# Attending the first batch whole before the feed-forward, with weights taken column by column

## The chip, the cores and the metric

The kernel runs on one core of one Trainium2 chip. The metric is the device time in microseconds (us). Most executions of a kernel agree within a few tenths of a per cent; a run that lies over 1.5% above the fastest of its kernel is called slow, and comparisons use the fast runs. TensorE's clock is at times halved; the records give the granted clock for any stretch, as a share of full speed (0.50 in some stretches below, the first from 44.90 to 51.73 us in the run with the old order). This record begins only when the clock is first released, at 10.71 us in the kernel before. What lies earlier is shown as 1.00, although the same pair of 503-column matmuls takes 1.05 us at 7.78 and 0.59 at 11.03.

## The reference

Two parts, one after the other, in float32:

```python
# 4 batches, 8 heads, 768 positions, 64 per head; 4 sink positions, window of 128
scores = q @ k.T / sqrt(64)
keep   = (key < 4) | ((query - key >= 0) & (query - key < 128))
a      = softmax(where(keep, scores, -1e9))
x      = (a @ v)                      # heads side by side: 3072 tokens x 512
out    = (relu(x @ w_gate) * (x @ w_val)) @ w_out     # 512 -> 1536 -> 512
```

Any token of the feed-forward needs all eight heads of its batch, so no feed-forward work on batch 0 can start before all heads of at least the first tokens are attended.

## The kernel before

It works in bf16. Attention goes in units of two heads. A unit is loaded, cast by GpSimd, transposed on TensorE (`T`), scored in groups of columns (`S`, exponential on ScalarE), multiplied with the values and the sums (`V`), and normalised on VectorE (`norm`). The feed-forward goes in chunks: one of 12 columns of weights for half a batch, 8 matmuls of 384 columns. The second product (`ffn2`) gathers 12 matmuls into one tile of 128 tokens.

```python
def chunk(b, c0, n, m):                     # first product, 4 + 4 matmuls
    for ko in range(KO):
        nc.tensor.matmul(out=gp, lhsT=wg[:, ko, m*128:(m+1)*128], rhs=x[:, ko, c0:c0+n], ...)
    nc.scalar.activation(gs, gp, Act.Relu)
    for ko in range(KO):
        nc.tensor.matmul(out=vp, lhsT=wv[:, ko, m*128:(m+1)*128], rhs=x[:, ko, c0:c0+n], ...)
    nc.vector.tensor_tensor(hT[:, m, c0:c0+n], gs, vp, op=Alu.mult)

def ffn2(b, t, m, tail=False):              # second product, one of 12 matmuls of a tile
    nc.tensor.matmul(out=op, lhsT=hTs[b][:, m, t*128:(t+1)*128], rhs=wo[:, m, :],
                     start=m == 0, stop=m == FM - 1)
    if m == FM - 1:
        nc.scalar.copy(ot[:], op)           # then stored
```

To start the feed-forward early, batch 0 is cut into two kinds of units, "L" (the first 376 tokens of two heads) and "M" (the other 392). The four L units come first, with filler matmuls ("warm") between them. The M units and the full "F" units of the other batches follow as stages between the chunks, at a pace given by PLAN (pairs of chunk number and stages done by then):

```python
for p in range(NP):                          # the front, cut
    U[p].S(0); ...; U[p].S(1)
    if p + 2 < NP: U[p + 2].T(*GV)
    warm(8)
    if p >= 1: norm(U[p - 1], 0, ps_gv)
...
ORDER = [(0, h, m) for h in range(2) for m in range(FM)]   # all 12 columns for one half, then the other
PLAN = ((0, 0), (2, 0), (10, 19), (23, 43), (47, 67), (71, 89), (72, 90))
for ci, (b, h, m) in enumerate(ORDER):
    while si < min(total, want(ci)):
        stages[si](); si += 1
    chunk(b, c0, n, m)
    left = FM - ci % FM
    for _ in range((len(f2) + left - 1) // left):   # second product spread evenly
        f2.popleft()()
```

Batch 0 gets its causal masks by an extra matmul before the scores; later batches by a multiplication on VectorE. The weights are loaded by GpSimd in four quarters of columns, the output weights in three thirds of rows, one third after the casts of each of three successive units.

The softmax here doesn't subtract the row's maximum and nothing guards it: scores larger than these inputs give would overflow.

## Time and profile before

The median is 276.26 us over four runs (275.64 to 277.87). Cutting the profiled span by TensorE's own timeline gives a table that the rest of this text uses. In the view of windows of the kernel before, each line has the stretch, its length, the busy time of each engine with its number of instructions (TensorE, weight load, VectorE, ScalarE, GpSimd), the granted clock, the DMA share and GB/s:

```profile
0.00:22.77 22.77, 17.71 (x189) 11.53 (x190) 12.84 (x37) 10.70 (x22) 19.18 (x45) 1.00 1.10 223
22.77:91.47 68.70, 63.52 (x653) 38.44 (x652) 48.28 (x113) 41.65 (x65) 32.03 (x53) 1.00 0.90 202
91.47:261.48 170.01, 170.01 (x1280) 94.73 (x1279) 86.49 (x180) 74.83 (x128) 16.59 (x26) 1.00 0.21 66
261.48:273.90 12.42, 8.58 (x40) 3.72 (x38) 0.55 (x1) 2.38 (x5) 0.00 (x0) 0.99 0.23 84
```

The first number is the stretch's length, the second TensorE's busy time; their difference is its idle time: 5.06, 5.18, 0 and 3.84 us. In the long third stretch TensorE never pauses. So there are two ways to win: take matmuls out, or take idle time out of the first 91 us.

### The profile page before, as it was taken

Reading aid. Unit: us, or ns where it says so; the run is one execution under the profiler, and the core shown is the slowest. Engines: PE = TensorE matmul, PEld = TensorE weight load, DVE = VectorE, ACT = ScalarE, POOL = GpSimd, SP = SyncE. Lnnn points to the kernel's source line nnn. Section 1 sums busy time; section 2 is a strip of 40 time slices with the busy share of each in tenths; the row PEclk is TensorE's granted clock in tenths of the full one; section 3 lists DMA queues with packets and bytes.
Section 4 is the critical chain, followed back from the end, with each engine's and each line's share of the span. In section 5 each row is a group of like instructions: output and inputs, shape, how many; then the busy total and the mean of one; then the engine's idle time right before and its main releaser. Section 6 shows DMA issues by size and latency. Waiting matters only on the chain.

```text
span 273.9 us, 5552 instructions
## 1 busy us (share of the span) xinstructions
PE 259.8 (95%) x2158; PEld 148.4 (54%) x2158; DVE 148.2 (54%) x329; ACT 129.6 (47%) x218; POOL 67.8 (25%) x123
## 2 busy tenths in 40 slices
PE   5997899899989999999999999999999999999994
PEld 4564555555545555555565555555655555555541
DVE  2486355778797755465666646565474722222210
ACT  3743656666646544536435363644535333323321
POOL 7973547653441330030402105000000000000000
PEclk9999999999999999999999999999999999999999
DMA  8999999998465170531707125101101110011122
GB/s 196 260 224 207 246 255 231 254 251 189 114 172 162 54 212 10 159 84 44 209 4 212 41 75 142 38 0 41 38 2 38 41 38 10 28 42 38 38 77 78
DMA packets 46858, 31.20 MB, mean 114 GB/s; under 512 B 28400, under 2 KB 43760, under 8 KB 46832
## 3 DMA queue, kind: packets, MB, share of 16 engines
q1 hardware_dynamic: 40224, 25.93, 34.2%
q0 software_dynamic: 5808, 4.72, 11.0%
q8 instruction: 17, 0.28, 0.4%
q10 hardware_dynamic: 800, 0.20, 0.3%
q14 instruction: 9, 0.07, 0.1%
HBM read 29.26 MB, written 6.29 MB: 130 GB/s over the span
## 4 chain that ended last, share of the span: by engine, by line
PE 84%; DVE 8%; ACT 3%; issue 1%; DMA 1%; POOL 1%; SPq 0%; DVEq 0%; ACTq 0%
PE gp L323 22%; PE op L342 22%; PE vp L329 21%; PE ops L248 7%; PE sps L226 5%; PE sps L221 2%; DVE R L311 2%; PE tkq L180 2%; DVE R L308 2%; PE tkq L183 2%; DVE xT L313 2%; ACT ee L230 2%; DMA stg<-in_q_dram 1%; DVE ee L232 1%; DVE rc L309 1%
## 5 line engine op out<-in xcount | busy, mean ns | idle before, releaser
L326 ACT ACTIVATE gs<-gp 128x384 f32<-128x384 f32 (+2 forms) x96 | 47.3, 493 | 73.2 <-PE gp L323 71.4
L323 PE MATMUL gp<-xT,wg 128*128 128x384 bf16 (+2 forms) x384 | 78.8, 327 | 1.4 <-DVE xT L313 1.4
L331 DVE TENSOR_TENSOR hT<-gs,vp 128x384 bf16<-128x384 f32 (+2 forms) x96 | 52.7, 549 | 49.3 <-PE vp L329 42.1
L329 PE MATMUL vp<-xT,wv 128*128 128x384 bf16 (+2 forms) x384 | 78.1, 326 | 0.0
L342 PE MATMUL op<-wo,hT 128*128 128x512 bf16 x288 | 75.9, 379 | 0.0
L230 ACT ACTIVATE ee<-sps 128x1006 bf16<-128x1006 f32 (+4 forms) x52 | 46.3, 905 | 26.5 <-PE sps L226 26.5
L329 PEld LDWEIGHTS <-wv 128*128 128x128 bf16 x384 | 37.6, 98 | 26.4 <-issue 1.6
L323 PEld LDWEIGHTS <-wg 128*128 128x128 bf16 x384 | 32.5, 98 | 25.2 <-issue 4.3
L342 PEld LDWEIGHTS <-hT 128*128 128x128 bf16 x288 | 28.2, 98 | 25.1
L232 DVE TENSOR_TENSOR ee<-ee,msk 128x1006 bf16<-128x1006 bf16 (+2 forms) x36 | 26.0, 723 | 26.0 <-ACT ee L230 25.8
L153 POOL CAST kn<-stg 128x768 bf16<-128x768 f32 (+2 forms) x20 | 15.4, 768 | 72.9 <-DMA stg<-in_k_dram 48.7
L346 ACT COPY ot<-op 128x512 f32<-128x512 f32 x24 | 14.1, 586 | 21.6 <-PE op L342 21.5
L308 DVE STREAM_TRANSPOSE R<-ops 128x384 f32<-128x384 f32 (+1 forms) x28 | 16.4, 584 | 14.3 <-PE ops L248 14.3
L186 ACT COPY kT<-tkq 128x768 bf16<-128x768 bf16 (+2 forms) x20 | 14.0, 700 | 18.1 <-PE tkq L183 17.9
L157 POOL CAST vn<-stg 128x768 bf16<-128x768 f32 (+2 forms) x20 | 14.4, 720 | 22.7 <-DMA stg<-in_v_dram 16.7
L311 DVE STREAM_TRANSPOSE R<-rc 128x384 f32<-128x384 f32 (+1 forms) x32 | 18.6, 582 | 1.1
L248 PEld LDWEIGHTS <-ones 128*64 128x64 bf16 x280 | 12.1, 109 | 12.3 <-issue 7.4
L313 DVE TENSOR_TENSOR xT<-ops,R 128x384 bf16<-128x384 f32 (+2 forms) x32 | 17.8, 557 | 1.4
L226 PEld LDWEIGHTS <-kT 64*128 64x128 bf16 x136 | 6.6, 93 | 19.2 <-issue 16.8
L248 PE MATMUL ops<-ee,ones 128*64 128x251 bf16 (+9 forms) x256 | 14.3, 238 | 2.2 <-DVE xT L313 1.3
L226 PE MATMUL sps<-qT,kT 64*128 64x251 bf16 (+3 forms) x136 | 15.5, 250 | 0.8 <-ACT qT L188 0.8
L153 POOL CAST qn<-stg 128x768 bf16<-128x768 f32 (+2 forms) x20 | 14.5, 724 | 5.2 <-DMA stg<-in_q_dram 4.8
(53 smaller groups left out, 169.8 us busy)
## 6 DMA issues: line engine op xcount, KB each, us to landing
out_dram<-ot SPq DMA_DIRECT2D x24, 256.0 KB
stg<-in_k_dram SPq DMA_DIRECT2D x12, 384.0 KB
stg<-in_q_dram SPq DMA_DIRECT2D x12, 384.0 KB
stg<-in_v_dram SPq DMA_DIRECT2D x24, 192.0 KB
wg<-in_moe_w_gate_dram POOLq DMA_DIRECT2D x4, 384.0 KB, 9.7
wv<-in_moe_w_val_dram POOLq DMA_DIRECT2D x4, 384.0 KB, 11.8
wo<-in_moe_w_out_dram POOLq DMA_DIRECT2D x3, 512.0 KB, 5.9
stg<-in_k_dram SPq DMA_DIRECT2D x4, 280.0 KB
```

The costliest lines, as they stand in the source:

```text
L153: cp(dst[0:pp, 0:nn, :, :], self.staging(what)[0:pp, :, :].rearrange("p h (n d) -> p n h d", d=64))
L226: nc.tensor.matmul(out=ps[:, h, c:c + w], lhsT=self.kw(j, r), rhs=qT[s][r, qa:qa + w], start=not biased, stop=True, skip_group_check=True)
L230: nc.scalar.activation(x, ps[:, :, 0:c], Act.Exp, bias=0.0, scale=scale)
L232: nc.vector.tensor_tensor(x, x, bc(msk[:, m0:m0 + c], 2), op=Alu.mult)
L248: nc.tensor.matmul(out=ps[1 - what][64 * h:64 * h + 64, qa - q0:qa - q0 + w], lhsT=self.vn[:, j, h, :] if what else ones[:], rhs=ee[s][:, ...
L311: nc.vector.transpose(r[:, 1, 0:w], bass.AP(a.tensor, a.offset, [a.ap[0], [1, nb], [0, 32]]))
L313: nc.vector.tensor_tensor(xTs[u.b][:, u.p, lo:hi], o[:, lo - c0:hi - c0], r[:, 1, lo - c0:hi - c0], op=Alu.mult)
L323: nc.tensor.matmul(out=gp[:, 0:n], lhsT=wg[:, ko, m * 128:(m + 1) * 128], rhs=x[:, ko, c0:c0 + n], start=ko == 0, stop=ko == KO - 1)
L326: nc.scalar.activation(gs[:, 0:n], gp[:, 0:n], Act.Relu, bias=0.0, scale=1.0)
L329: nc.tensor.matmul(out=vp[:, 0:n], lhsT=wv[:, ko, m * 128:(m + 1) * 128], rhs=x[:, ko, c0:c0 + n], start=ko == 0, stop=ko == KO - 1)
L331: nc.vector.tensor_tensor(hT[:, m, c0:c0 + n], gs[:, 0:n], vp[:, 0:n], op=Alu.mult)
L342: nc.tensor.matmul(out=op, lhsT=hTs[b][:, m, t * 128:(t + 1) * 128], rhs=wo[:, m, :], start=m == 0, stop=m == FM - 1)
```

## The change

The front now attends batch 0 whole in full units, and does the first three steps of the next unit, before the first chunk. These are 28 of the 98 stages (a unit has six: three score groups, the norms of two halves, and the transposes of the next unit). The M and L units go, and with them the fillers but 16. The chunks of batch 0 take three weight columns for both halves before the next three, so that each quarter of the weights serves six chunks. The second product takes up to three matmuls a chunk. The core of the diff (cut: everything that removes the L and M geometry, and the loads):

```diff
-        U = [Unit(p, 0, p, "L") for p in range(NP)] + [Unit(NP + p, 0, p, "M") for p in range(NP)]
-        U += [Unit(2 * NP + (b - 1) * NP + p, b, p, "F") for b in range(1, B) for p in range(NP)]
+        U = [Unit(i) for i in range(B * NP)]
 ...
             def v():
+                if prev is not None:
+                    norm(prev, 1, ps_at if on_array else ps_gv)
             def t():
                 if nxt is not None:
+                    nxt.T(not on_array)
+                    nxt.sinkk()               # two VectorE copies of key columns into kTs
+                if x == 0:
+                    load_w(0)
+                    load(5)
+                elif x == 1:
+                    load_w(1)
+                elif x == 3:
+                    load_w(2)
+                    load(6)
+                elif x == 4:
+                    load_w(3)
+                    load(7)
+                elif 5 <= x:
+                    held(x + 3)
+                    if x < 8:
+                        load_wo(x - 5)
                 if at(x + 3) is not None:
                     casts(at(x + 3), "kqv")
+            return [s(0), v, s(1), t, s(2), lambda: norm(u, 0, ps_at if on_array else ps_gv)]
 ...
-        ORDER = [(0, h, m) for h, m in [(h, m) for h in range(2) for m in range(FM)]]
+        ORDER = [(0, h, m) for g in range(0, FM, 3) for h in range(2) for m in range(g, g + 3)]
-        PLAN = ((0, 0), (2, 0), (10, 19), (23, 43), (47, 67), (71, 89), (72, 90))
+        PLAN = ((0, 28), (24, 50), (48, 74), (71, 98))
 ...
-            left = FM - ci % FM
-            for _ in range((len(f2) + left - 1) // left):
+            for _ in range(min(3, len(f2))):
                 f2.popleft()()
```

## The prediction

> **What bounds the kernel now.** I read first the page's busy times and its 40 slices, then the chain that ended last, then TensorE's timeline piece by piece, because "busy" can hide slack.
>
> ```profile
> span 273.9 us, 5552 instructions
> PE 259.8 (95%) x2158; PEld 148.4 (54%) x2158; DVE 148.2 (54%) x329; ACT 129.6 (47%) x218; POOL 67.8 (25%) x123
> ...
> PE   5997899899989999999999999999999999999994
> ...
> DMA  8999999998465170531707125101101110011122
> ...
> PE 84%; DVE 8%; ACT 3%; issue 1%; DMA 1%; POOL 1%; SPq 0%; DVEq 0%; ACTq 0%
> ```
>
> TensorE carries the chain (84%), no other engine passes 54%, and the DMA engines are full only in the first ten slices, about 68 us. So the time is TensorE's work at its pitch, plus what it waits, plus the start. The timeline of TensorE (start, length, line, shape, count) gives the pitches and the start:
>
> ```profile
> 7.78 1.05 PE L221 MATMUL sps<-bias,ident 128*128 128x503 bf16 x2
> ...
> 11.03 0.59 PE L221 MATMUL sps<-bias,ident 128*128 128x503 bf16 x2
> ...
> 19.63 1.07 PE L370 MATMUL warm<-ident 128*128 128x128 bf16 x16
> 20.76 0.64 PE L323 MATMUL gp<-xT,wg 128*128 128x376 bf16 x3
> 22.77 0.32 PE L323 MATMUL gp<-xT,wg 128*128 128x376 bf16 x1 [1.38 <-DVE xT L313]
> ...
> 78.30 0.53 PE L248 MATMUL ops<-ee,ones 128*64 128x119 bf16 x10 [0.66 <-DVE xT L313]
> ...
> 91.47 0.82 PE L323 MATMUL gp<-xT,wg 128*128 128x384 bf16 x4
> ...
> 228.37 0.81 PE L342 MATMUL op<-wo,hT 128*128 128x512 bf16 x3
> 229.01 0.81 PE L323 MATMUL gp<-xT,wg 128*128 128x384 bf16 x4
> ...
> 261.48 8.58 PE L342 MATMUL op<-wo,hT 128*128 128x512 bf16 x39
> ```
>
> I split the 273.9 us in four. (1) The front: half of batch 0 (the "L" units) is attended and the first chunk of the feed-forward really runs from 22.77. Until then TensorE mostly runs 70 filler ("warm") matmuls. (2) From 22.77 to 91.47: 24 chunks, 24 second-product matmuls, the second half of batch 0 (the "M" units) and 26 stages of full units. Waits are marked here: the ten longest sum to 5.2 us, like the 0.66 shown. (3) From 91.47 to 261.48, 170.0 us, no wait is marked. (4) 39 second-product matmuls and 3.8 us of copy and store after the last.
>
> Part 3 gives unit prices. A chunk is 8 matmuls of 384 columns, 1.30 us from start to start (229.01 to its op at 230.31). Three second-product matmuls take 0.64 (228.37 to 229.01), so 0.215 each. The stretch holds 72 chunks (93.6) and 225 second-product matmuls (288 less 24 before and 39 after; 48.4); the 28.0 left is 47 attention stages, 0.60 each, so 3.6 us for a unit of six.
>
> [...] while weights load (12 to 40 us) the weight queue moved 500 to 750 packets in each 4 us, about as many as or half as many as the load queue. So a weight load that starts early slows the heads' loads.
>
> **The change part by part.**
>
> Removed: the L and M units with 16 L and M stages inside the chunks; 54 of the 70 fillers; the even spreading of the second product. Kept: 96 chunks, 288 second-product matmuls. Added: 28 stages (four full batch-0 units with masks added by matmul, and two score groups and a norm step around unit 4) before the first chunk. Moved: weights are needed a quarter at a time, six chunks apart instead of three.
>
> After the first chunk, at T1: 96 x 1.30 = 124.8; 288 x 0.215 = 61.9; 70 remaining stages (98 in all less 28) x 0.60 = 42.0; the end 3.8. Sum 232.5. For before, the same sum from 22.77 is 251.1 (its 273.9 less 22.77), of which 4 M units are about 11.6 (2.9 each: transposes 0.45, mask matmuls 0.68, scores 0.65, values 0.85, switches), full stages 73 x 0.60 = 43.8, and waits 5.2. So after T1 the change saves about 18.6 less its own waits, and the question is how late T1 is.
>
> T1, by engines, for one unit with measured means: ScalarE copies kT and qT 0.80 + 0.81, exps 1.01 + 1.01 + 0.87: 4.5 us. VectorE two norms of 0.58 + 0.23 + 0.58 + 0.56, and the sink copies 0.29 + 0.20: 4.4. GpSimd casts 0.83 x 3 + 0.31 + 0.53: 3.3. TensorE 3.6 + mask matmuls 2 x 1417 columns[...], 1.2: 4.8. DMA, from the packet records: k and q 512 packets of 1536 B at 74 ns, v 1584 packets of 256 B at 21 ns, over 16 engines: 2.4 + 2.1 = 4.5. Nothing dominates; all need 4.4 to 4.8, and the hand-overs decide.
>
> Walk: k of unit 0 lands at about 3.7 and is cast by 4.6. q comes on ScalarE's queue at about 4.7, cast by VectorE by 5.6. Transposes end at 6.2, the copies at 7.1, unit 0's first exp starts at 8.0. From then the order on ScalarE (exp0, exp1, kT, qT of the next unit, exp2), with score group 0 of the next unit waiting for qT, gives about 5.0 us a unit: first exps at 8.0, 13.2, 18.0, 22.9. Unit 0 runs partly at half clock; [...] I expect release at 10 to 13.
>
> Unit 4's transposes must come before the first chunk. By engine order they could run at 25.0. Their data: units 0 to 3 are 18 us of DMA from 1.8. GpSimd issues the first weight quarter behind unit 2's v cast (about 16.4 to 17.9), and that is 1024 packets at 78 ns over 16 engines, 5.0. Unit 4's k and q add 2.4. 25.4 in all; two queues overlap (34.6 us of packet time went in 28 us of 12 to 40, a ratio of 1.2), so they land at about 24 to 25. But GpSimd must first cast unit 3's v and issue the next weights (until about 25.1), then cast k and q: 26.8. So transposes at 26.8, not 25.0; then copies, scores, V of unit 3, second scores: 4.2 us. T1 = 31.0.
>
> Waits after T1: for 21 chunks no second product fills, a stage and a chunk are 1.9 us at 0.92 stages a chunk, VectorE needs 0.92 x 1.1 + 0.55 = 1.6 of it. Before had its 5.2 at up to 1.5 stages a chunk. I take 3.0, including some of T(5), whose data come at 32 to 35 beside the second weights, against a need at about 35. Weights 2 to 4 are needed near 42, 53, 64, and land by 33, 49, 56: no wait. The output weights' last third is issued when GpSimd is done with unit 9 (about 72) and is needed near 79: none.
>
> Sum: 31.0 + 232.5 + 3.0 = 266.5 of span. The reported median lies 2.8 above the profiled span (276.72 against 273.9): 269.3. Semaphore hand-overs in the walk are counted thinly, so I add 0.5: **269.8 us**.
>
> The second product: three a chunk end a tile of 12 on every fourth chunk's boundary, so the one PSUM buffer has 1.3 us for its 0.59 us copy. 225 are done in the chunks from the 22nd on and 63 are left behind the last chunk, against 39. That only moves work: TensorE is full either way and the tail uses two buffers in turn. Value 0. The spread of before (2, 4, 3 a chunk) had no marked wait on this buffer, so nothing to win.
>
> **The rivals.**
>
> A: the front is DMA-bound. For: slices 1 to 10 of DMA are at 8 or 9 tenths; the weights take two thirds of the engines while they load; a full unit needs 1.19 MB where an L unit needs 0.59. Against: k and q come in 1536 B rows instead of 768 and 1024. If unit 4's k and q land at 30, T1 is about 35, and unit 5 waits too: 274 to 276, within 2%.
>
> B: TensorE stays at half clock in the front, with its fillers gone. A unit is then 9.6 us on TensorE, T1 about 45, and the time 282 to 285, slower. [...]
>
> C: before's marked waits don't come back at all and the hand-overs in the front are as thin as walked: T1 29.2 and waits 1: 265.5.
>
> D: only the start moves and stalls return elsewhere (VectorE, which must take norms of unit 3 and masks of unit 4 as the first chunks arrive): waits 6: 272.5.
>
> **Range and chances.** C to A spans 265 to 275, and I take that as the range. The 2% line is 271.2; I put 0.64 below it, 0.32 within 2%, and 0.04 on B or a missed hazard.
>
> **What would show it.** Right: the first gp matmul near 31; the pair of 503-column matmuls at 0.59 by the second unit; no fillers after 4; the last wait before T1 at unit 4's transposes, named GpSimd's cast; 24 chunks afterwards with fewer marked waits than 5.2; about 63 second-product matmuls in the last piece. Wrong: T1 past 35; a named DMA wait on the weights in a gp matmul; pairs of 503 columns still above 1 us after 14; VectorE in front of TensorE for more than 6 us in all.

## The result, and the profile after

The changed kernel takes 266.73 us, the median of four runs (265.70 to 272.48; the last one is a slow run with a granted clock of 0.992). Before took 276.26. The ratio is 0.9634, with a 95% interval of 0.9572 to 0.9696: faster. A ratio here is taken from fast runs alone, so it is not quite the ratio of the medians.

The page of the kernel after (the span, the busy times, the slices and the chain's shares), from the run of 266.43 us:

```profile
span 264.6 us, 5333 instructions
PE 255.0 (96%) x2088; PEld 143.9 (54%) x2088; DVE 147.2 (56%) x318; ACT 126.6 (48%) x202; POOL 64.1 (24%) x102
...
PE   3989999999999999999999999999999999999994
...
DMA  7999999988391614308071341011011011111132
...
PE 87%; DVE 8%; DMA 2%; ACT 1%; issue 1%; POOL 0%; DVEq 0%; ACTq 0%
```

TensorE still carries the chain. Its busy time fell from 259.8 to 255.0 us. The timeline of TensorE, kernel after, at the places that answer to those shown of before:

```profile
7.35 1.05 PE L174 MATMUL sps<-bias,ident 128*128 128x503 bf16 x2
...
12.84 0.60 PE L174 MATMUL sps<-bias,ident 128*128 128x503 bf16 x2
...
14.43 0.28 PE L179 MATMUL sps<-qT,kTs 64*128 64x248 bf16 x2 [0.78 <-DVE kTs L160]
...
26.60 0.49 PE L151 MATMUL tk<-ident,kn 128*128 128x128 bf16 x6
...
30.93 0.81 PE L275 MATMUL gp<-xT,wg 128*128 128x384 bf16 x4
...
32.01 0.81 PE L281 MATMUL vp<-xT,wv 128*128 128x384 bf16 x4 [0.27 <-DVE R L260]
...
246.61 14.41 PE L294 MATMUL op<-wo,hT 128*128 128x512 bf16 x66
```

The first chunk starts at 30.93. In the kernel before, the first three of its eight matmuls ran at 20.76, and it went on at 22.77, where the windows are cut. Only the 0.27 us at 32.01 is marked as a wait between it and 60 us. The last group holds 66 second-product matmuls, 63 behind the last chunk and that chunk's own 3. The windows of the kernel after, cut to match those of before:

```profile
0.00:30.93 30.93, 25.23 (x308) 15.84 (x309) 21.39 (x57) 20.65 (x25) 20.51 (x40) 1.00 1.10 258
30.93:90.00 59.07, 58.72 (x521) 34.27 (x522) 43.63 (x94) 33.36 (x54) 26.93 (x37) 1.00 0.83 181
90.00:246.60 156.60, 156.60 (x1194) 87.47 (x1193) 81.68 (x168) 69.06 (x117) 16.63 (x25) 1.00 0.21 65
246.60:264.60 18.00, 14.42 (x68) 6.34 (x65) 0.55 (x1) 3.57 (x7) 0.00 (x0) 0.97 0.23 87
```

TensorE's idle time is now 5.70, 0.35, 0 and 3.58 us. Against before that is +0.64, -4.83, 0 and -0.26, so -4.5 in all; the busy time is 4.85 less; together they are the 9.3 us by which the span fell (273.9 to 264.6). In other words: the front is 8.2 us longer, but it is filled with work instead of fillers, and the rest is 17.4 us shorter (251.1 to 233.7), because the extra work of the M units and three full stages are gone from it and it hardly waits any more.

### The profile page after: what moved, and what is told of

Its sections match the earlier page's. It is cut to its first block, busy times and chain, and to the rows that moved or that the text cites. A ratio compares the mean times of both kernels' runs of the same rounds, so it can differ in the third digit from the quotient of the medians.

```text
span 264.6 us, 5333 instructions
## 1 busy us (share of the span) xinstructions
PE 255.0 (96%) x2088; PEld 143.9 (54%) x2088; DVE 147.2 (56%) x318; ACT 126.6 (48%) x202; POOL 64.1 (24%) x102
## 4 chain that ended last, share of the span: by engine, by line
PE 87%; DVE 8%; DMA 2%; ACT 1%; issue 1%; POOL 0%; DVEq 0%; ACTq 0%
PE gp L275 25%; PE op L294 23%; PE vp L281 23%; PE ops L201 7%; PE sps L179 4%; PE tkq L151 3%; DVE R L263 2%; DVE xT L265 2%; DMA stg<-in_k_dram 2%; DVE R L260 1%; DVE kTs L159 1%; DVE kTs L160 1%; DVE rc L261 1%; ACT kT L153 1%; ACT ee L183 0%
## 5 line engine op out<-in xcount | busy, mean ns | idle before, releaser
L278 ACT ACTIVATE gs<-gp 128x384 f32<-128x384 f32 x96 | 47.2, 492 | 66.1 <-PE gp L275 65.7
L275 PE MATMUL gp<-xT,wg 128*128 128x384 bf16 x384 | 78.7, 328 | 0.0
L281 PE MATMUL vp<-xT,wv 128*128 128x384 bf16 x384 | 78.1, 326 | 0.4 <-DVE R L260 0.3
L283 DVE TENSOR_TENSOR hT<-gs,vp 128x384 bf16<-128x384 f32 x96 | 52.6, 549 | 41.4 <-PE vp L281 33.3
L183 ACT ACTIVATE ee<-sps 128x1006 bf16<-128x1006 f32 (+2 forms) x48 | 46.2, 965 | 29.9 <-PE sps L179 29.9
L260 DVE STREAM_TRANSPOSE R<-ops 128x384 f32<-128x384 f32 x24 | 14.0, 583 | 11.9 <-PE ops L201 11.7
L263 DVE STREAM_TRANSPOSE R<-rc 128x384 f32<-128x384 f32 x32 | 18.5, 578 | 1.1
L265 DVE TENSOR_TENSOR xT<-ops,R 128x384 bf16<-128x384 f32 x32 | 17.8, 557 | 1.7
L201 PE MATMUL ops<-ee,vn 128*64 128x255 bf16 (+8 forms) x288 | 15.5, 233 | 0.4 <-DVE xT L265 0.3
L179 PE MATMUL sps<-qT,kT 64*128 64x251 bf16 (+2 forms) x128 | 14.9, 255 | 0.1
```

Source lines behind the costliest of these rows:

```text
L179: nc.tensor.matmul(out=ps[:, h, c:c + w], lhsT=self.kw(j, r), rhs=qT[s][r, qa:qa + w], start=not self.biased, stop=True, skip_group_check= ...
L183: nc.scalar.activation(x, ps[:, :, 0:c], Act.Exp, bias=0.0, scale=scale)
L201: nc.tensor.matmul(out=ps[1 - what][64 * h:64 * h + 64, qa - q0:qa - q0 + w], lhsT=self.vn[:, j, h, :] if what else ones[:], rhs=ee[s][:, ...
L263: nc.vector.transpose(r[:, 1, 0:w], bass.AP(a.tensor, a.offset, [a.ap[0], [1, nb], [0, 32]]))
L265: nc.vector.tensor_tensor(xTs[u.b][:, u.p, c0:c0 + w], o[:, 0:w], r[:, 1, 0:w], op=Alu.mult)
L275: nc.tensor.matmul(out=gp[:, 0:n], lhsT=wg[:, ko, m * 128:(m + 1) * 128], rhs=x[:, ko, c0:c0 + n], start=ko == 0, stop=ko == KO - 1)
```

## The experiments

The theory after the result was: the gain is what the prediction says, real work in a start that cannot be made short, and it holds because three things arrive in time (the units' casts, the weights' quarters and the output weights), which the order of the chunks and the pace of the stages were laid out for. Rivals: the second product's burst of three is what gains; the pace of the stages doesn't matter; the front is bound by loads alone. One rival was not run: the kernel before with only its full units brought at an even pace, which would show how much of the gain needs the new front. Runs of one chip may be compared with each other; the kernel before took 276.2 to 277.0 on every chip. All results were correct.

### The order of the chunks back to one half after the other

```diff
-        ORDER = [(0, h, m) for g in range(0, FM, 3) for h in range(2) for m in range(g, g + 3)]
+        ORDER = [(0, h, m) for h in range(2) for m in range(FM)]
-            for _ in range(min(3, len(f2))):
+            for _ in range(min(3, len(f2)) if ci >= 21 else 0):
```

(The second product is held back as in the changed kernel, so that only the order differs.)

> The changed kernel with batch 0 taken token-half-major again (twelve chunks of the first half, then twelve of the second); the second product is still held back to the 22nd chunk, so only the need for weights moves. Theory (the column-major order is what lets the weights come late): the third weight quarter is issued at 38.7 to 40.2 us and in the changed kernel's packets is complete at about 47.5; the 7th chunk would want it at about 42. Wait of 4 to 7 us at the 7th chunk, little at the 10th, total 4 to 7 us longer than the changed kernel. Rival (the weights are hidden anyway, the order is tidiness): within 0.5 us of it.

Measured on chip 7: 272.98 us (271.42 to 273.47), ratio 0.9855 (0.9823 to 0.9887). TensorE's timeline and the window after it:

```profile
44.97 1.46 PE L275 MATMUL gp<-xT,wg 128*128 128x384 bf16 x4 [2.29 <-DMA wg<-in_moe_w_gate_dram]
...
47.78 1.46 PE L281 MATMUL vp<-xT,wv 128*128 128x384 bf16 x4 [1.35 <-DMA wv<-in_moe_w_val_dram]
```

```profile
44.90:51.73 6.83, 5.42 (x19) 1.99 (x20) 1.51 (x3) 1.99 (x3) 3.45 (x6) 0.50 1.29 207
```

Two waits on a weight quarter, 3.64 us together, and the clock at half for 6.83 us from the end of the first on, which costs up to 3.4 more (an estimate, half of 6.83). The four matmuls take 1.46 us instead of 0.81. From the first chunk to the end it took 240.3 us instead of 233.7. So the new order is what lets the weights come late, and without it this stretch took 6.6 us longer. The marked waits alone are under the 4 to 7 us expected; with the halved clock the total falls within it. The total is only 1.6 us longer than that of the changed kernel on the same chip (271.40, below), because that one has a wait of its own there, which this kernel has not: totals alone would have misled here.

### The second product spread evenly again

```diff
+            left = FM - ci % FM
-            for _ in range(min(3, len(f2))):
+            for _ in range(min(3, len(f2)) if ci < 24 else (len(f2) + left - 1) // left):
```

> The changed kernel with the second product from the 25th chunk on spread evenly over what is left of a token half (the rule of the kernel before) instead of three a chunk. It comes out at 6 a chunk, then 3, and the tail falls from 63 to about 36 matmuls. Theory: moving TensorE work is worth nothing, but with 9 already done, groups of 6 put the end of a tile of 12 in the middle of a chunk's group five times; the next tile then waits for the one PSUM buffer's copy, 0.59 us and the hand-over, so 5 waits of 0.5 to 0.9 us: 2.5 to 4.5 us longer than the changed kernel. Rival 1 (prediction, value 0 in any arrangement): within 0.5 us. Rival 2 (the longer tail of 63 costs): 1 us or more shorter.

Measured on chip 7: 272.75 us (271.71 to 275.86), ratio 0.9894 (0.9843 to 0.9945). The last group has 39 matmuls again. One of five like waits on TensorE's timeline:

```profile
81.96 0.81 PE L294 MATMUL op<-wo,hT 128*128 128x512 bf16 x3 [0.67 <-ACT ot L298]
```

With what is queued by then, the even spread takes six matmuls a chunk. The tiles no longer end where a chunk begins: after three of the six one tile ends, the next needs the one PSUM buffer at once, and waits for the copy out of it, five times 0.67 us. Unit 5's casts were waited for too (0.46 and 1.35 us) and the output weights 0.55 us. So in this schedule the spread of before would have cost time; the burst of three isn't a gain by itself but avoids that loss.

### The same rule in the kernel before

Two runs on the old kernel, which has its second product spread evenly: first three a chunk throughout, then two a chunk until chunk 24 and three from there.

```diff
-            left = FM - ci % FM
-            for _ in range((len(f2) + left - 1) // left):
+            for _ in range(min(3, len(f2))):                          # first
+            for _ in range(min(3 if ci >= 24 else 2, len(f2))):       # second
```

> The kernel before with the second product taken three a chunk, nothing else: one part of the change alone. Theory: three a chunk ends every tile of 12 on a chunk's boundary, as the 2, 4 and 3 a chunk of the kernel before also did, so nothing is won or lost: within 0.5 us of the kernel before, with more than 39 matmuls in the last piece. Rival (three a chunk carries part of the gain, by relieving the PSUM buffer or ScalarE): 1 us or more faster.

> The kernel before with the second product two a chunk until the 24th chunk (as it had) and three a chunk after it, so that the output weights are in before they are needed, which e8 did not ensure. Theory (the arrangement of the second product is worth nothing once its weights are there and its tiles end on chunk boundaries; e8's 7 us were waits for those weights and the halved clock behind them): within 0.7 us of the kernel before, no marked wait on the output weights. Rival (three a chunk itself costs or wins): more than 1 us either way without such a wait.

The first, on chip 7, took 283.77 us (281.16 to 284.11), ratio 1.0234 (1.0193 to 1.0275). I had expected no change, and missed. TensorE's timeline:

```profile
61.41 0.59 PE L342 MATMUL op<-wo,hT 128*128 128x512 bf16 x2 [1.05 <-DMA wo<-in_moe_w_out_dram]
...
69.59 0.38 PE L342 MATMUL op<-wo,hT 128*128 128x512 bf16 x1 [4.59 <-DMA wo<-in_moe_w_out_dram]
```

Three a chunk reaches the second and the last third of the output weights before they have come: 5.64 us of waits, and after the longer one 3.41 us at half clock. The loads themselves moved too: the last third was issued at 64.02 us instead of 59.31, since the casts ahead of it on GpSimd had waited for a unit's values. The second run, which takes only two a chunk until the weights are there, took 276.52 us on chip 14 (275.84 to 277.90), ratio 1.0016 (0.9988 to 1.0043), without such a wait. So "value 0" holds for the number three itself, and it is the arrival of the output weights that it must not outrun.

### The pace of the stages

The new PLAN brings the stages of batch 1 evenly over 24 chunks; the old one brought up to 24 in 13 chunks. This run brings them in a burst again, in the changed kernel:

```diff
-        PLAN = ((0, 28), (24, 50), (48, 74), (71, 98))
+        PLAN = ((0, 28), (8, 32), (21, 52), (24, 54), (48, 74), (71, 98))
```

> The changed kernel with the attention stages bunched: 4 stages in chunks 1 to 8, then 20 stages in 13 chunks (1.54 a chunk, the rate that the kernel before had from its 11th to its 24th chunk), then 2 in 3. Same instructions. Theory (the waits of the kernel before came from VectorE at that rate): marked TensorE waits of 0.4 to 0.7 us each on VectorE's norm come back, 2 to 5 us in all, total 2 to 5 us longer. Rival (they came from the halves of batch 0, not from the rate): no waits, within 0.5 us.

Measured on chip 7: 269.37 us (269.12 to 269.73), ratio 0.9735 (0.9711 to 0.9760). The timeline shows waits again like those of the kernel before, on the normalisation of a unit:

```profile
49.54 0.49 PE L151 MATMUL tkq<-ident,kn 128*128 128x128 bf16 x6 [0.54 <-DVE xT L265]
...
59.35 0.49 PE L151 MATMUL tkq<-ident,kn 128*128 128x128 bf16 x6 [0.99 <-DVE xT L265]
...
69.15 0.49 PE L151 MATMUL tkq<-ident,kn 128*128 128x128 bf16 x6 [0.98 <-DVE xT L265]
```

With the first chunk at 30.91, the rest took 236.6 us of span instead of 233.7: +2.9, of which these three and one of 0.40 are 2.91. So the pace costs that much by itself: at 1.5 stages a chunk (20 stages over 13 chunks) VectorE is behind, at 0.92 (22 over 24) it isn't. It is not the whole of what before lost. The old PLAN brought 24 stages in those 13 chunks, 1.85 a chunk and not the 1.5 that the prediction and this expectation name. And of its ten marked waits (5.19 us) six, 2.75 us, lie before 50 us, at the M units, and three of these are put down to ScalarE; they went with the M units. The other four, 2.44 us on norms, are the ones that this run speaks of.

### The same kernel again, and the output weights earlier

The runs on chip 7 were all slower than the profile of the changed kernel had led me to expect, so the changed kernel itself was run there.

> The changed kernel unchanged, as control for the small differences of this call and to see its slow runs. Expected 265.5 to 267.5 us in most runs and, if the theory of the next run holds, some of 269 to 273 us that carry a lowered mean clock (0.99).

It took 271.40 us (268.90 to 273.54), ratio 0.9793 (0.9751 to 0.9835), unclear at 2%; none of its six runs lay in the 265.5 to 267.5 us that I had expected of most. Its timeline:

```profile
77.85 0.59 PE L294 MATMUL op<-wo,hT 128*128 128x512 bf16 x2
80.46 0.38 PE L294 MATMUL op<-wo,hT 128*128 128x512 bf16 x1 [2.02 <-DMA wo<-in_moe_w_out_dram]
```

The ninth second-product matmul is the first to use the last third of the output weights. In the good run of the result that third was issued at 71.18 us and used at 77.42: a load took 6.0 us from issue to landing (the median of the three), so the margin was 0.2 us. Here it was issued at 72.88, 1.70 us later, because the unit's queries came 2 us later to the cast ahead of it; and it took 7.5 us to land (the shortest of the three loads), while it was needed 0.86 us later. Together that is the wait of 2.02 us. Then the same kernel with the second and the last third each loaded one unit earlier:

```diff
                     held(x + 3)
-                    if x < 8:
-                        load_wo(x - 5)
+                    if x == 5:
+                        load_wo(0)
+                        load_wo(1)
+                    elif x == 6:
+                        load_wo(2)
```

> The changed kernel with the second part of the output weights issued one unit earlier (at unit 5) and the third at unit 6 instead of 7. Theory: the changed kernel's spread (265.7 to 272.5) comes from the third part: it is issued at 71.2 us and first used at about 77.6, so when it lands late TensorE waits 1 to 2 us[...]. Expected: all runs within 265 to 267.5, none with a mean clock under 0.996, median 0 to 1 us under the control. Rival (the slow runs are a state of the chip): the same share of slow runs as in the control.

> The same kernel as e6 (output weights issued a unit earlier), as control for the next run and to see whether e6 repeats. Expected 265.5 to 267.5 us median; not more than a third of the runs above 268.5.

On chip 7: 267.16 us (265.64 to 269.20), ratio 0.9660 (0.9618 to 0.9702), 4.2 us below the control. The last issue is at 62.72, the wait is gone. Not all of the difference is this wait: the profiled runs differ by 3.8 us of span, of which the wait is 2.02, and 1.12 is a first chunk that came earlier (29.82 against 30.94), which the change does not touch. On chip 14: 266.83 us (265.79 to 267.49), ratio 0.9655 (0.9631 to 0.9678). There its trace has no wait for the output weights either; it has one of 1.73 us for unit 5's cast, at 35.40. The control's profiled run has a wait of 2.02 us and no halved clock, but five of its six runs have a mean clock of 0.987 to 0.994. One halved stretch of 3.41 us, as in the run with the reductions below (behind a wait of 1.94 us on the output weights), would make 0.994 (half of 3.41 is 0.6% of 267), two 0.987; an estimate, as those runs have no trace. Two runs of the mended kernel on chip 7 were also at 0.994 and 269 us, against what I had expected (none over 267.5), so the clock was lowered there at times with this kernel too; by what, stays open.

### Three attempts on the front

The first taken alone: the sink columns' two copies as reductions over an axis of one element. What made me think of it is VectorE's timeline of the kernel after, and GpSimd's at the same time:

```profile
12.36 1.33 DVE L159 COPY kTs<-kT 128x372 bf16<-128x372 bf16 x1 [3.86 <-ACT kT L153]
13.61 0.76 DVE L160 COPY kTs<-kT 128x12 bf16<-128x12 bf16 x1
```

```profile
12.73 0.82 POOL L127 CAST kn<-stg 128x768 bf16<-128x768 f32 x1
13.52 0.83 POOL L127 CAST qn<-stg 128x768 bf16<-128x768 f32 x1
```

The long copy ends at 13.69, within 0.15 us of the first cast's end (13.55), and the short one at 14.37 with the second cast's (14.35). Undisturbed they take 0.29 and 0.15 to 0.20 us (unit 4's pair, at 28.50 and 28.69: 0.28 and 0.15). The prediction had counted the undisturbed times. In the run with the early weights, below, a copy of 12 columns took 2.20 us. That a reduction would not be drawn out beside a cast was my estimate; no trace had shown it before this run.

```diff
+            for dst, from_ in ((kTs[s][:, 0:3, 4:128], band), (kTs[s][:, 0:3, 0:4], first4)):
+                if self.i < 5:
+                    one = bass.AP(from_.tensor, from_.offset, [*from_.ap, [1, 1]])
+                    nc.vector.tensor_reduce(out=dst, in_=one, axis=mybir.AxisListType.X, op=Alu.max)
 ...
```

> The changed kernel with the sink copies of units 0 to 4 on VectorE written as a reduction over an axis of one element[...]. Theory[...]: each pair of copies takes about 0.45 plus 0.1 to 0.2 us[...], instead of up to 1.33 plus 0.76; VectorE's first norm starts at about 12.9 instead of 14.3, the first chunk at 29.5 to 30.3 instead of 30.9, total 0.6 to 1.4 us shorter. Rival (the copies are slow for another reason, or the front is bound by ScalarE or the loads): copies still over 1 us, or first chunk unmoved within 0.3 us.

Measured on chip 7: 269.35 us (265.63 to 270.14), ratio 0.9688 (0.9641 to 0.9736); its profiled run was a slow one. VectorE's timeline, and TensorE's further on:

```profile
12.46 0.61 DVE L163 TENSOR_REDUCE kTs<-kT 128x372 bf16<-128x372 bf16 x2 [3.96 <-ACT kT L153]
```

```profile
79.54 0.38 PE L299 MATMUL op<-wo,hT 128*128 128x512 bf16 x1 [1.94 <-DMA wo<-in_moe_w_out_dram]
```

The pair takes 0.61 us for each of the five units. The first chunk came at 30.53, against 30.94 in the control: a unit took 4.91 us instead of 5.1 to 5.2, with ScalarE then waiting 0.84 us for the next scores. In this run the clock was also released late (12.55 us). And the wait of 1.94 us on the output weights was followed by 3.41 us at half clock. So the pair, up to 2.01 us as copies beside GpSimd's casts (12.36 to 14.37), takes 0.61 as reductions. What that is worth is not shown: the 0.4 us at the first chunk is less than what it moves with an unchanged front (29.14 to 30.94 us), the front was read from a slow run, and the totals (269.35 against 271.40) also carry waits on the output weights.

Second, the first quarter of the weights issued after unit 0's casts, to see whether the loads are what the front stands on:

```diff
         casts(U[0], "v")
+        load_w(0)
         casts(U[1], "kqv")
 ...
                 if x == 0:
-                    load_w(0)
                     load(5)
```

> The changed kernel with the first weight quarter issued by GpSimd after unit 0's casts (about 9 us) instead of after unit 2's (16.8 us). Theory (the loads have only 1 to 4 us of slack against the order of the engines in the front): unit 2's q lands and is cast about 3 to 5 us later, its transposes move from 16.5 to 18.5 to 20, and the first chunk from 30.9 to 32.5 to 34.5; total 1.5 to 3.5 us longer. Rival 1 (front bound by the engines, loads far ahead): first chunk within 0.5 us of 30.9. Rival 2 (the front is bound by the loads outright): the full 5 us of the quarter's transfer, first chunk at 35.5 or later.

Measured on chip 7: 270.13 us (269.08 to 271.71), ratio 0.9763 (0.9721 to 0.9805). The first chunk came at 33.01, with TensorE waiting 1.06 us for unit 1's cast of k; after it the rest took 235.8 us, with a wait of 1.91 us on the output weights. So the units of the front have no slack for a weight load this early: 2.1 us were lost (33.01 against 30.94, the latest of the unchanged front). The total does not show the loss that I had expected: it is 1.3 us below the control (271.40), most of whose runs had a lowered clock (0.987 to 0.994) where three of the four here had 1.000.

Third, everything that should shorten the front together: the early output weights, the reductions, both score groups ahead of the previous unit's norm, and 40 fillers instead of 16:

```diff
-        warm(16)
+        warm(40)
 ...
-            return [s(0), v, s(1), t, s(2), ...]
+            first3 = [s(0), s(1), v] if x < 4 else [s(0), v, s(1)]
+            return [*first3, t, s(2), ...]
```

> e9 with three changes of the front together: the sink copies of units 0 to 4 as one-element reductions[...], the second score group of the batch-0 units put before the norm of the unit ahead, and 40 instead of 16 filler matmuls at the start[...]. Theory (with the copies free of GpSimd the front's period is ScalarE's 4.9 us with a 0.84 us wait for the second score group, then VectorE's 4.75): period 4.7 to 4.8 us, unit 0 about 0.5 us earlier, first chunk at 29.0 to 30.0 us; total 0.5 to 1.5 us shorter than e9, if unit 5's loads, which then are needed earlier, don't take it back. Rival (the loads or the stages after the first chunk take it back): first chunk earlier but total within 0.5 us of e9, with a marked wait on GpSimd's cast for unit 5.

Measured on chip 14: 269.98 us (269.69 to 271.01), ratio 0.9779 (0.9758 to 0.9801). It's 3.1 us longer than the kernel with only the early output weights (266.83). The clock was released at 7.17 us (9.94 in the other) and the first chunk came at 28.71, 1.1 us before the other's 29.82. Then TensorE's timeline and the window:

```profile
33.95 0.51 PE L151 MATMUL tkq<-ident,kn 128*128 128x128 bf16 x6 [1.81 <-POOL kn L127]
...
35.54 0.82 PE L151 MATMUL tkq<-ident,qn 128*128 128x128 bf16 x6 [1.09 <-POOL qn L127]
```

```profile
34.48:41.31 6.83, 5.77 (x27) 2.94 (x28) 2.72 (x4) 3.25 (x5) 5.79 (x9) 0.50 1.08 301
```

Unit 5's casts come no sooner: GpSimd takes them behind unit 4's values, and those were there only at 30.97 (29.78 in the other kernel), so unit 5's k was cast from 33.07 (32.29). The faster front runs into 2.90 us of waits, with the clock at half for 6.83 us from just after the first of them. More was given back than won.

### The version put together

The last run keeps the faster front and moves unit 5's transposes from the third chunk to the seventh, so that its casts have time:

```diff
-        PLAN = ((0, 28), (24, 50), (48, 74), (71, 98))
+        PLAN = ((0, 28), (6, 29), (24, 50), (48, 74), (71, 98))
```

> e10 with one more change: unit 5's transposes, which found their data late in e10 (2.9 us of marked waits and 6.83 us of halved clock), are put at the 7th chunk instead of the 3rd, and the stages behind them follow at 1.17 instead of 0.92 a chunk. Theory (e10 lost its earlier start only to unit 5's loads): first chunk at 28.5 to 29.5 us, no marked wait for GpSimd's casts of unit 5, no halved clock after release, total 263 to 265.5 us, below e9 by 1.5 to 3.5 us. Rival 1 (the loads are late for the next units or weights instead): a marked wait on GpSimd's cast or on a weight transfer of over 1 us moves to units 6 to 8 or to the 13th chunk, total 266 us or more. Rival 2 (VectorE at the faster stage rate): waits of over 1.5 us on VectorE in all.

Measured on chip 13: 266.23 us (265.36 to 267.70), ratio 0.9636 (0.9612 to 0.9660), all six runs fast, no halved clock. That misses what I had expected. The waits on unit 5 are gone but the stages now come up late at the other end; on TensorE's timeline:

```profile
78.45 0.32 PE L280 MATMUL gp<-xT,wg 128*128 128x384 bf16 x1 [1.24 <-DVE xT L270]
```

That is batch 1's first chunk waiting for the norm of its last unit's first half, done one chunk later than in the changed kernel. The first chunk came at 29.54 us and the rest took 235.0. So it equals the changed kernel's good runs, and the kernel with only the early output weights (266.83 on chip 14). It is not shown to be faster, nor steadier: the slow runs were seen on chip 7, and this kernel ran on chip 13 alone, where the changed kernel did not run. One more stage by chunk 24 might win the 1.24 us; that was not run.

## Why the prediction was right

The time came out at 266.7 us inside the range of 265 to 275, and on the side of over 2% faster that had 0.64. It lies near the range's lower end, 3.1 us under the 269.8 that was named: the gain was forecast at 6.9 us (from 276.72) and measured at 9.5. The sum, term by term: the profiled run took 266.43 us.

| term | predicted | measured |
|---|---|---|
| first chunk (T1) | 31.0 | 30.93 |
| from the first chunk to the end | 235.5 (232.5 at unit prices, 3.0 of waits) | 233.7 |
| run less span | 2.8 | 1.8 (266.43 less 264.6) |
| allowance for hand-overs | 0.5 | none |
| sum | 269.8 | 266.43 |

The third line was a slip: the prediction set the median of three runs, 276.72, beside the span of another, faster run. That run took 275.65 us, so run less span was 1.8 before as well.

**The unit prices.** Chunk, second product and stage were priced from start to start in the stretch without waits. They gave 232.5 of the 233.7 us, and the 1.2 left over contains all waits (TensorE's idle time before the tail is 0.35). This is the step that carried the prediction. That the M units' extra, three full stages and the waits would go (18.6 us with none left) is borne out: the stretch became 17.4 us shorter. One reading of the start was wrong without harm: TensorE did not "mostly" run fillers there; they are 6.38 of its 17.71 busy us.

**T1.** It was right by two errors that cancelled. The walk through the engines was too early from the start: unit 0's k was cast from 5.22 us on, where I had it landed at 3.7 and cast by 4.6, and the first exponentials of units 0 to 3 came at 9.21, 14.75, 19.90 and 24.97, not 8.0, 13.2, 18.0 and 22.9. Part of it is the short copies that ran beside GpSimd's casts (1.33 and 0.76 us where I counted 0.29 and 0.20, and TensorE waited 0.78 us for them at 14.43). Against that I had let unit 4's transposes wait for GpSimd until 26.8. Its casts in fact started at 22.89 and were done at 24.5, and the transposes at 26.60 are not marked as waiting: they came by engine order. The sign that I had named for this step, a wait on GpSimd's cast before T1, did not show. That T1 isn't sharply determined is seen in the runs with the same front, where it lay between 29.14 and 30.94. Two things go with it. The copies of units 1 to 3 take 2.84 us in all where it is 29.14, 3.34 and 3.48 where it is 29.82, and 4.24 to 4.58 where it is 30.60 to 30.94. And the clock is released at 9.45 in the first, at 9.94 and 10.86 in the next two, and at 10.77 to 11.99 in the rest. The run with the reductions has the copies at 1.83 but the release at 12.55, and its first chunk at 30.53. So the copies are not the whole of it, and the two were not tried apart.

**Waits after T1.** I took 3.0, and at most 1.2 came. That fewer stages a chunk mean fewer waits is borne out by the run with the burst (2.91 us of waits on VectorE); the size was too large for the profiled run. In the control the marked waits after the first chunk do come to 2.97 us, but 2.02 of them are the output weights', for which the prediction had none. The wait for T(5), unit 5's transposes, that it included came in some runs (0.68 us in the control, 1.73 on chip 14, 1.81 in the even spread) and not in others.

**The weights.** "Weights 2 to 4 ... no wait" was right, and the run in the old order shows what else would have come: 3.64 us of waits and a halved clock. "The output weights' last third is issued when GpSimd is done with unit 9 (about 72) and is needed near 79: none" was right in the profiled run by 0.2 us only (issued 71.18, landing about 6.0 later, needed 77.42). In the control on chip 7 the same program waited 2.02 us for it. That is the step that was weak: it compared two times with no spread, and didn't ask what a wait would lead to. Its sum had no term for a halved clock behind a wait, as in the run with the reductions (1.94 us of wait, then 3.41 us at half clock).

**The second product.** "Value 0" holds where the weights are there (the old kernel at two and then three a chunk: 1.0016), and fails in either direction otherwise: three from the start in the old kernel cost 2.3%, through the weights, and the old spread in the new schedule cost waits on the PSUM copy.

**The rivals.** A, a front bound by DMA, didn't come, though the front stands close to it: one early weight quarter cost 2.1 us of T1, and the faster front was stopped by unit 5's late data. B, half clock in the front, did not come: the pair of 503 columns is at 0.60 us by 12.84. C, thin hand-overs and no waits (265.5), came nearest to the result: its waits of 1 are what came, while its first chunk at 29.2 came only in the run with the even spread (29.14). D, stalls that return elsewhere, did not come in the profiled run; it came in part in the control, as said, and when a run changed the pace or the order.

**What waits did to the clock.** In the traces single waits of 1.81 (faster front), 1.94 (reductions), 2.29 (old order) and 4.59 us (three a chunk in the kernel before) were followed by half clock, but others of 1.73 (early output weights, chip 14), 1.91 (early weights) and 2.02 us (control) were not. So the length of a wait alone does not tell them apart. In the four runs half clock began at 34.48, 80.81, 44.90 and 70.13 us. Over the 3.41 us before that, TensorE was busy for 1.50, 1.47, 1.19 and 0.54 us. The faster front's, as the view of windows has it:

```profile
31.07:34.48 3.41, 1.50 (x12) 0.62 (x9) 2.19 (x4) 0.49 (x1) 2.68 (x4) 1.00 1.26 241
```

The half clock lasted 3.41 us in the run with the reductions and in that with three a chunk, and 6.83 us in the old order and the faster front, where a second wait (1.35 and 1.09 us) fell into its first 3.41 us. What decides whether half clock follows a wait is not shown; no run was made to test it. Of 3.41 us at half clock up to 1.7 are lost (an estimate, half of 3.41), so that the wait of 1.94 us can have cost nearly twice its length.

## What to carry to other kernels

Price work by its pitch, from start to start, in a stretch without waits. Fill a start that cannot be made short with work that must be done, and order the use of the weights so that they may come late. A transfer that lands with no margin is a risk, not a zero (a margin of 0.2 us in the profiled run, a wait of 2.02 us in the control): half clock may follow its wait (3.41 us of it behind 1.94 us in the run with the reductions), and a front made faster only counts when what follows is also ready.
